# Copying the norms of q and k to SBUF so that GpSimd can scale q and k, with the whole order table replaced

## The chip, the cores and the metric

One core of one Trainium2 chip runs the whole kernel as one program. The metric is the device time of one execution in microseconds; three runs are shown. The engines are named as in the profile: PE (TensorE, with PEld for its weight loads), DVE (VectorE), ACT (ScalarE), POOL (GpSimd) and SP (SyncE, which here only issues DMAs). "f16 pair" below means a float32 value that is held as a float16 part and a float16 rest, so that PE can multiply at float16 speed without losing the precision.

## The reference

Attention over 8 batches, 12 heads, 448 positions and 64 columns, with an RMS norm of q and k ahead of it, then a mixture of experts over the 3584 rows that result.

```
q_n = q / sqrt(mean(q*q, -1) + 1e-6) * g_q        # k_n likewise, with g_k
attn = softmax(q_n @ k_n.T / sqrt(64)) @ v
x = attn as (3584, 768)
group g = argmax(x @ w_group), 4 groups
expert e = argmax(x @ w_expert[g]), 4 in a group
out = softmax weight of g * softmax weight of e * (relu(x @ w1[g, e]) @ w2[g, e])     # inner width 1024
```

## The kernel before

**Work.** Attention runs in 16 units of six heads each (half a batch). A unit's q and k are loaded as 21 blocks of 64 columns on 128 partitions (1344 elements a partition). `plan_prep` prepares a unit: ACT squares (`sq`), DVE sums (`red`, L285), ACT takes the power -1/2 by Ln and Exp (`rs1`, L291 and L292, which writes 42 numbers a partition into PSUM, into unused columns of a bank `po`), DVE refines them by a Newton step (`rs2`, L296 to L298, in the same place). Then DVE multiplies k and q by their norms (`norm`, L301): k in place in two pieces of 896 and 448 elements, q into the buffer `qp` in two pieces of 704 and 640. ACT makes the float16 part of k (`k_hi`, L312), POOL or DVE the rest (`k_lo`, L316, tile `kn`), PE transposes k and q (`pkt` L321, `pqt` L342), and ACT and DVE bring them back to SBUF. The first unit does this in three pieces of 448 (`plan_first`).

`plan_max` finds the row maxima (PE `pmx` L544, DVE `mx` L554), `plan_scores` the scores (PE `pss` L623), their exponentials (ACT `p` L633) and the float16 rest `pl` of each (L639, on POOL or DVE), and `plan_av` multiplies with v (PE `po` L684). Ninety per cent of the 177 `pl` operations take 896 elements. `plan_finish` splits a unit's output into an f16 pair (`xhl`, L751) and stores it.

The second half routes rows to 16 experts and runs them in 18 jobs. An expert's weights are loaded as float32 in 8 pieces of 768 KB (`stage<-w`), split by ACT into a float16 part (`w1h`, `w2h`, L1407) and by DVE into the rest (`w1l`, `w2l`, L1409), and used by PE (`ps` L1458 and L1485). POOL gathers rows (`xg`, L1447), SP transposes them by DMA (`mx<-xg`, L1558).

**What sets the order.** Every step up to the tenth expert job is a task of `Flow`. A table `PLAN` holds one number for each task, in the order in which the tasks are made; tasks are issued in the order of these numbers, and a star picks the second of the engines that the task allows. Each engine then works through its own queue in that order and waits where data, a buffer or a semaphore is missing. The numbers are read for the order alone (and for the places of the later jobs among them).

**One of the two at a time.** Tasks marked by `shared` (L108) are operations of DVE or POOL that read SBUF in a way that the program keeps apart: where a marked DVE task was issued last, the next marked POOL task waits for it by a semaphore (`emit`, L112). It does not make DVE wait for POOL.

Of the kernel before, what the change touches and what calls it, by code (L numbers as in the profile page):

```python
# [59 lines left out]
class Task:  # L60
    def __init__(self, engines, f, deps, takes, uses):
        self.engines, self.f, self.deps, self.takes, self.uses = engines, f, deps, takes, uses
        self.port = False


class Flow:
# [41 lines left out]
    def shared(self, task):  # L108
        task.port = True
        return task  # L110

    def emit(self, agenda, step):  # L112
# [18 lines left out]
class Attention:  # L131
# [7 lines left out]
    ROOM = dict(nk=2, nq=2, nv=2, sq=2, ss=1, qp=1, kn=1, qh=1, kt=3, kb=3, qa=3, qb=3, vh=3, vl=3, mx=2, mxt=2,  # L139
# [121 lines left out]
    def plan_prep(self, flow, u, B, D):  # L261
# [133 lines left out]
        if u == 0:  # L395
            self.plan_first(add, D, B, N, dict(
                sq=sq, red=red, rs1=rs1, rs2=rs2, norm=norm, k_hi=k_hi, k_lo=k_lo, k_tr=k_tr, k_ev=k_ev, k_cp=k_cp, q_one=q_one, q_out=q_out,
                q_dup=q_dup, rms=rms, fl=fl), both, d)
        else:
# [22 lines left out]
            for a, e in HV:  # L422
                n = (e - a) * self.D
                nq.append(add("DVE", lambda a=a, e=e: norm_q(a, e), [y, *nq],
                              takes=[B["qp"]] if a == 0 else (), uses=[B["nq"], B["ss"]] + ([B["qp"]] if a else [])))
# [35 lines left out]
    def plan_first(self, add, D, B, N, F, both, d):  # L461

        fl, rms = F["fl"], F["rms"]
# [10 lines left out]
        for i in range(NPR):  # L474
# [7 lines left out]
            for nm, o in (("k", N), ("q", 0)):  # L482
# [5 lines left out]
            x = add("DVE", (lambda a=a, e=e: F["norm"](fl(d["k"])[:, a:e], fl(d["k"])[:, a:e], rms()[:, N + a:N + e]))  # L488
                    , [y], uses=[B["nk"], B["ss"]])
            nq = add("DVE", (lambda a=a, e=e: F["norm"](fl(d["q"])[:, a:e], fl(d["q"])[:, a:e], rms()[:, a:e])),  # L490
                     [y, x], uses=[B["nq"], B["ss"]])
# [274 lines left out]
    def plan(self, flow, router, order):  # L766
# [15 lines left out]
        for u in range(U):  # L782
            D = {}
            B = {n: Buffer(n, True) for n in ("nk", "nq", "ss", "qp", "kn", "qh")}
# [37 lines left out]
class Router:  # L822
# [177 lines left out]
    def plan(self, flow, a, e, stores, done, room, logits=None):  # L1000
# [5 lines left out]
        d = {}  # L1006
# [95 lines left out]
        for j in range(19):  # L1102
# [3 lines left out]
            x.port = on == "POOL" or j in (1, 3, 5, 6, 12, 15, 18)  # L1106
# [592 lines left out]
1 0 2406 430 1069 2636 9806 12318 12312 708 2073 2 130 550 611 709 710 741 805 1055 1057 1101 1638* 1807 1986 1116  # L1699
1271 1658 1455 2796 210 340 711 792 791 857 922 1181 1296 1402 1362 1775* 1910 2175 1563 1657 3409 1772 4477 612 742  # L1700
864 1056 1054 1115 1180 1272 1349 1561 1562 1912* 2234 2458 1637 1911 2456 2072 4830 1351 2635 4509 2722 4875 2174
# [3 lines left out]
5401 5468 5587 5612 5669 5820 6018 6474 6051 6113 6278 6345 6432 6612 6663 7677 7983* 6943 6944 7033 7275 7277 7367  # L1705
# [4 lines left out]
9606 8050 8174 8337 8404 8539 8598 8743 9184 9577* 8561 8639 9008 9010 9180 9182 9354 9607 10331 9615 9672 10327 10329  # L1710
10336 10340 10344 10744 10805* 11016 11217 12143 2177 2342 2514 2855 2854 3043 3327 3410 3509 3726 3830 3604 3933 4176
3831 4476 4047 4175 4349 4445 6249 4829 4874 4988 5368 5584 5588 5590 5745 5582 5821 7368 7602 10332 7414 7603 7678
8723 8742 9007 7979 8049 8149 8287 8383 8451 8450 8538 8638 7759 7812 9013 9025 9357 9578 9673 10333 10334 10335 10405
9709 9814 10330 10404 10505 10604 10609 10659 10929 10345 10424 10661* 10633 10740 11275 11336 11437 11582 11436 11490
11671 11947 12043 12142 11862 11971 12044 10607 10742 10804 10871 10928 11096 11276 11581 11624 11015 11219 11277
11491 11625 11763 11811 12611 12970* 11910 12045 12316 12374 12460 12594 12706 13497 13668 13684 13980 14761 3832 3178
4054 4523 3812 4828 4832 4915 5108 5467 6162 5204 5585 6434 6049 6433 7035 7113 7617 7756 7320 8540 6734 6841 7034
7031 7032 7278 8289 6942 7676 9440 10346 10660 10605 12372 10328 10337 10338 10965 11218 11220 10342 10347 10606 10754
10831 11017 11221 11235 11335 10608 10741 11585 11761 12313 12384 12500 12969* 12315 12317 12968 12497 12593 12971
12777 12886 13114 12863 12967 13326 12939 13057 13156 13059 13138 13496 13927 14019 14123 14124 14129 14293 14297  # L1720
14465 14620 14519 14577 14760 13498 13670 13674 13676 13680 13687 13771 13978 14296* 13678 13682 13734 13852 14295
14336 14464 14703 15469 14480 14557 14682 14825 14938 15051 15139 15468 15717* 15923 16226 16627 5589 4831 6383 6662
# [10 lines left out]
19906 19563 19565 19860* 17955 18062 18397 18525 18567 18684 18751 19107 19342* 18908 19008 19108 19114 19151 19285  # L1733
# [161 lines left out]
```

## Time and profile before

| | |
|---|---|
| three runs | 983.2, 984.35, 988.45 us; median 984.35 |
| the profiled execution, whole | 988.83 us |
| its span, first to last instruction | 987.1 us |
| PE busy | 899.2 us (91% of the span) |
| DVE busy | 727.5 us (74%) |
| ACT busy | 615.1 us (62%) |
| POOL busy | 540.4 us (55%) |
| mean granted TensorE clock | 0.976 of full speed (2.4 GHz) |

A busy share over the whole span mixes the two halves: attention fills the engines other than PE up to about 470 us, the experts' weights fill the DMA queues after it. So the rows below are by stretch. In a row of the view by stretches each engine's busy time and number of instructions stands first, then the granted clock, the share of the 16 DMA engines and the rate. In a row of the view by groups the numbers after the bar are the busy time of all, the mean of one in ns, and the engine's idle time just before them with what ended it.

### The profile page before, as it was taken

What the parts mean: (1) busy time and instruction counts of PE and PEld (TensorE: products, weight loads), DVE (VectorE), ACT (ScalarE), POOL (GpSimd) and SP (SyncE); (2) the same over time, 40 slices, a digit from 0 to 9 for tenths busy, and PEclk for the clock granted to TensorE, in tenths of its full rate; (3) what the DMA queues carried; (4) which work ended last, traced back from release to release, by engine and by line L of the source; (5) the groups of instructions that cost most, each with busy time, mean ns of one, the idle gap of its engine ahead of it and who ended that gap; (6) DMA issues with size and microseconds to landing.
All of it is one profiled execution on the core that took longest, in us unless ns stands there. A gap on an engine that the chain in (4) does not pass through costs nothing.

```text
span 987.1 us, 28670 instructions
## 1 busy us (share of the span) xinstructions
PE 899.2 (91%) x11761; PEld 647.7 (66%) x11761; DVE 727.5 (74%) x1017; ACT 615.1 (62%) x950; POOL 540.4 (55%) x445
## 2 busy tenths in 40 slices
PE   2789989999998999987989999999879999999997
PEld 2356656666665665655857767667667777878885
DVE  5999989899998999899743656565547685756530
ACT  6779888889988886746441644555426555536521
POOL 7489989989999898677243423112212231424411
PEclk9699999999999999989999999999989999999999
DMA  6775878878789955449999999999988899999920
GB/s 174 186 174 143 204 162 209 165 200 195 191 186 185 222 137 105 113 97 275 240 231 245 279 302 231 286 302 317 252 298 213 299 291 304 323 253 278 293 77 29
DMA packets 222071, 213.82 MB, mean 217 GB/s; under 512 B 128410, under 2 KB 178598, under 8 KB 221937
## 3 DMA queue, kind: packets, MB, share of 16 engines
q1 hardware_dynamic: 213456, 188.46, 74.2%
q0 software_dynamic: 7584, 23.04, 7.5%
q8 instruction: 93, 1.52, 0.7%
q10 hardware_dynamic: 896, 0.46, 0.2%
q14 instruction: 42, 0.34, 0.1%
HBM read 145.69 MB, written 23.41 MB: 171 GB/s over the span
## 4 chain that ended last, share of the span: by engine, by line
PE 37%; DMA 21%; DVE 16%; issue 8%; POOL 6%; ACT 5%; SPq 4%; POOLq 0%; ACTq 0%; DVEq 0%
PE ps L1458 15%; PE ps L1485 12%; DMA mx<-xg 8%; DVE mx L554 5%; POOL pl L639 4%; DMA xg<-x,tb 3%; PE po L684 3%; DMA stage<-w 3%; PE pss L623 3%; ACT p L633 2%; DVE pl L639 2%; DMA qa<-qh 1%; DMA nk<-k 1%; DMA vn<-v 1%; DMA rx<-x 1%
## 5 line engine op out<-in xcount | busy, mean ns | idle before, releaser
L639 POOL TENSOR_TENSOR pl<-p 128x896 f16<-128x896 f32 (+1 forms) x151 | 250.2, 1678 | 38.2 <-ACT p L633 13.9
L1458 PE MATMUL ps<-mx,w1h 128*128 128x256 f16 (+6 forms) x1728 | 246.4, 258 | 18.5 <-DVE hl L1467 9.7
L1458 PE MATMUL ps<-mx,w1l 128*128 128x256 f16 (+6 forms) x864 | 212.3, 258 | 0.0
L554 DVE TENSOR_REDUCE mx<-pmx 128x2 f32<-128x896 f32 (+1 forms) x177 | 174.6, 1033 | 9.5 <-PE pmx L544 6.6
L1458 PEld LDWEIGHTS <-w1h 128*128 128x128 f16 x1728 | 156.2, 99 | 38.3 <-issue 21.9
L633 ACT ACTIVATE p<-pss 128x896 f32<-128x896 f32 (+1 forms) x177 | 152.1, 882 | 46.2 <-PE pss L623 31.8
L684 PEld LDWEIGHTS <-p 128*128 128x128 bf16 (+1 forms) x3072 | 144.1, 102 | 52.3 <-issue 36.8
L684 PE MATMUL po<-vh,pl 128*128 128x65 f16 (+1 forms) x1536 | 156.0, 196 | 15.2 <-POOL pl L639 11.5
L1485 PE MATMUL ps<-w2h,hh 128*128 128x384 f16 (+2 forms) x768 | 163.9, 305 | 3.2 <-ACT y L1497 3.2
L1485 PE MATMUL ps<-w2l,hh 128*128 128x384 f16 (+2 forms) x768 | 163.7, 304 | 0.0
L1485 PE MATMUL ps<-w2h,hl 128*128 128x384 f16 (+2 forms) x768 | 163.5, 304 | 0.0
L684 PE MATMUL po<-vh,p 128*128 128x65 f16 (+1 forms) x1536 | 158.7, 198 | 3.8 <-DVE po L298 1.3
L684 PE MATMUL po<-vl,p 128*128 128x64 f16 (+1 forms) x1536 | 157.1, 194 | 0.0
L1409 DVE SCALAR_TENSOR_TENSOR w2l<-stage,w2h 128x1536 f16<-128x1536 f32 x64 | 111.6, 1752 | 57.6 <-ACT w2h L1407 57.5
L1504 POOL DMA_INDIRECT out<-y,tb x23 | 33.9, 1473 | 215.1 <-ACT y L1497 97.1
L1409 DVE SCALAR_TENSOR_TENSOR w1l<-stage,w1h 128x1536 f16<-128x1536 f32 x64 | 112.9, 1786 | 48.4 <-ACT w1h L1407 48.4
L1485 PEld LDWEIGHTS <-hh 128*128 128x128 f16 (+2 forms) x1536 | 101.2, 100 | 60.6 <-issue 8.3
L684 PEld LDWEIGHTS <-pl 128*128 128x128 f16 (+1 forms) x1536 | 127.5, 102 | 19.1 <-POOL pl L639 14.8
L1465 ACT ACTIVATE hh<-ps 128x256 f16<-128x256 f32 (+6 forms) x144 | 47.4, 348 | 124.2 <-PE ps L1458 107.4
L1407 ACT ACTIVATE w2h<-stage 128x1536 f16<-128x1536 f32 x64 | 94.0, 1478 | 47.3 <-DMA stage<-w 47.3
L1407 ACT ACTIVATE w1h<-stage 128x1536 f16<-128x1536 f32 x64 | 93.4, 1478 | 44.2 <-DMA stage<-w 44.0
L1447 POOL DMA_INDIRECT xg<-x,tb x41 | 57.4, 1401 | 94.6 <-DMA mx<-xg 57.6
(208 smaller groups left out, 1575.6 us busy)
## 6 DMA issues: line engine op xcount, KB each, us to landing
stage<-w SPq DMA_DIRECT2D x64, 768.0 KB
stage<-w SPq DMA_DIRECT2D x64, 512.0 KB
stage<-w SPq DMA_DIRECT2D x64, 256.0 KB
vn<-v SPq DMA_DIRECT2D x16, 576.0 KB
x<-xhl SPq DMA_DIRECT2D x16, 576.0 KB
nk<-k SPq DMA_DIRECT2D x30, 288.0 KB
nq<-q SPq DMA_DIRECT2D x30, 288.0 KB
qa<-qh SPq DMA_DIRECT2D x30, 176.0 KB
```

The source lines that it names most:

```text
L554: nc.vector.tensor_reduce(d["mx"][:, a:ns[-1] + 1:step], d.pop(("mm", a))[:, 0:len(ns), 0:448], axis=AX.X, op=ALU.max)
L623: nc.tensor.matmul(s[:, n - a, 0:448], w[:, n * P:(n + 1) * P], mv[:, x:z], start=first, stop=not first)
L633: nc.scalar.activation(p[:, 0:e - a], s, AF.Exp, scale=1.0 / 64)
L639: ENG[eng].tensor_tensor(l[:, 0:n], p[:, 0:n], h[:, 0:n], op=ALU.subtract)
L684: nc.tensor.matmul(o[op, c, 0:nn], w, mv, start=st, stop=sp, skip_group_check=True)
L1407: self.nc.scalar.activation(hi, t, AF.Copy, scale=64.0)
L1409: self.nc.vector.scalar_tensor_tensor(lo, t, 64.0, hi, op0=ALU.mult, op1=ALU.subtract)
L1447: self.nc.gpsimd.indirect_dma_start(g[0:m], None, self.x16[0:n], bass.IndirectOffsetOnAxis(ap=tb[0:m, i, 0:1], axis=0), bounds_check=n - 1 ...
L1458: nc.tensor.matmul(s[:, 0:c], wb[w][:, i, fs], x[:, l + i, o:o + c], start=i + j == 0, stop=i == DC - 1 and j == 2)
L1465: self.nc.scalar.activation(hh, s[:, 0:c], AF.Relu)
L1485: nc.tensor.matmul(s[q * m:q * m + m, 0:n], self.h[h][:, f, a:a + m], wb[w][:, f, o:o + n], start=f + j == 0, stop=f == self.FC - 1 and j ...
L1504: i = self.nc.gpsimd.indirect_dma_start(out, bass.IndirectOffsetOnAxis(ap=idx, axis=0), d.pop(("y", i))[:, 0:self.D // r], None, bounds_ch ...
```

## The change

**The norms.** After `rs2`, ACT copies the 42 norms from PSUM to a new SBUF tile `z` (`rs3`, 18 copies: one a unit, three in the first). A scaling of q or k may now run on POOL, which multiplies by `z`, or on DVE, which multiplies by the numbers in PSUM as before and does not read `z`. A scaling on POOL waits for the last marked DVE task; a scaling on DVE isn't one that POOL waits for.

```
+    ROOM = dict(nk=2, z=2, ...
...
+        def rs3(a=0, e=N):
+            if "z" not in d:
+                d["z"] = self.wk.tile([P, 2 * N], F32, tag="z", name=f"z{u}", bufs=2)
+            nc.scalar.activation(both_(d["z"], a, e), both_(rms(), a, e), AF.Copy)
+
+        def norm(eng, dst, src, a, z):
+            y = (rms() if eng == "DVE" else d["z"])[:, a:z]
+            ENG[eng].tensor_tensor(dst, src, y.unsqueeze(2).to_broadcast([P, y.shape[1], self.D]), op=ALU.mult)
...
             y = add("DVE", rs2, [x], uses=[B["ss"]])
+            y = add("ACT", rs3, [y], takes=[B["z"]], uses=[B["ss"]])
...
-                nk.append(add("DVE", lambda a=a, e=e: norm_k(a, e), [y], uses=[B["nk"], B["ss"]]))
+                nk.append(flow.shared(add(both[::-1], lambda g, a=a, e=e: norm_k(g, a, e), [y], uses=[B["nk"], B["ss"], B["z"]]), "POOL"))
...
-            if t.port and t.on == "DVE":
+            if t.on == "DVE" and "DVE" in t.port:
                 held[:] = [i for i in seen if i.engine == mybir.EngineType.DVE][-1:]
-            elif t.port and held:
+            elif t.on == "POOL" and "POOL" in t.port and held:
...
 PLAN = """
-1 0 2406 430 1069 2636 9806 12318 12312 708 2073 2 130 550 611 709 710 741 805 1055 1057 1101 1638* 1807 1986 1116
...
```

**What the new table picks.** Twelve of the 66 scalings go to POOL: two of 448 elements in unit 0 (k and q), 448 of k and 704 of q in unit 1, all four in unit 2, 704 of q in units 3 and 8, 640 of q in units 5 and 14. Of `pl`, 11 go from POOL to DVE (nine of 896 elements, two of 448) and 9 from DVE to POOL (eight and one). Of `k_lo`, POOL gains one piece of 448 net. Three outputs `y` of the experts go from ACT to DVE. All other operations stay what they were; nearly all stand in another place.

**POOL, between the first unit's preparation and its first `pl`.** `qp` is the scaled q, `nk` k, `kn` the float16 pair of k, `z` the copied norms; the numbers behind the names (as in `kn_337`) tell buffers apart. Before:

```order
L316 TENSOR_TENSOR kn_337<-nk_237,kn_337 128x14x64
L316 TENSOR_TENSOR kn_337<-nk_237,kn_337 128x7x64
L316 TENSOR_TENSOR kn_474<-nk_320,kn_474 128x14x64
L316 TENSOR_TENSOR kn_474<-nk_320,kn_474 128x7x64
L639 TENSOR_TENSOR pl_0_536<-p_0_535 128x896
```

And in the changed kernel:

```order
L307 TENSOR_TENSOR qp<-nq_254,z_352 128x11x64
L322 TENSOR_TENSOR kn_370<-nk_238,kn_370 128x14x64
L307 TENSOR_TENSOR nk_238<-nk_238,z_352 128x448
L203 MEMSET kb_118 64x1344
L204 MEMSET kb_118 1x1344
L322 TENSOR_TENSOR kn_370<-nk_238,kn_370 128x7x64
L307 TENSOR_TENSOR nk_344<-nk_344,z_446 128x896
L307 TENSOR_TENSOR nk_344<-nk_344,z_446 128x448
L307 TENSOR_TENSOR qp<-nq_332,z_446 128x11x64
L322 TENSOR_TENSOR kn_473<-nk_344,kn_473 128x14x64
L307 TENSOR_TENSOR qp<-nq_332,z_446 128x10x64
L322 TENSOR_TENSOR kn_473<-nk_344,kn_473 128x7x64
```

Two scalings of unit 1 and all four of unit 2 now stand on POOL ahead of its first `pl`, and the second unit's `kn` stands behind three of them.

**DVE, the same place** (`ss` and `po` are `rs2` of unit 2, `mx` a row maximum, `ql` the rest of q). Before:

```order
L298 SCALAR_TENSOR_TENSOR po_112<-ss_392,po_112 128x42
L554 TENSOR_REDUCE mx_347<-pmx_20_434 128x1
L301 TENSOR_TENSOR nk_320<-nk_320,po_112 128x896
L301 TENSOR_TENSOR nk_320<-nk_320,po_112 128x448
L354 SCALAR_TENSOR_TENSOR ql_437<-pqt_1_451,ghc,qh_436 128x384
L301 TENSOR_TENSOR qp<-nq_339,po_112 128x11x64
L554 TENSOR_REDUCE mx_347<-pmx_16_469 128x2
```

And now:

```order
L298 SCALAR_TENSOR_TENSOR po_112<-ss_419,po_112 128x42
L563 TENSOR_REDUCE mx_368<-pmx_20_425 128x1
L360 SCALAR_TENSOR_TENSOR ql_444<-pqt_0_428,ghc,qh_443 128x1024
L360 SCALAR_TENSOR_TENSOR ql_444<-pqt_1_448,ghc,qh_443 128x384
L563 TENSOR_REDUCE mx_368<-pmx_14_467 128x2
```

The three scalings between `rs2` and the next row maximum are gone from DVE.

**DVE, where attention ends** (`pl15_18` is the `pl` of the last unit's blocks 18 and 19, `w1l0` the rest of the first expert's weights, `roh`, `rd`, `rc` and `rq` belong to the router). Before:

```order
L1409 SCALAR_TENSOR_TENSOR w1l0_9555<-stage3_9562,w1h0_9554 128x1536
L1046 TENSOR_TENSOR roh21_10036<-rd21_9812 128x48
L1409 SCALAR_TENSOR_TENSOR w1l0_9555<-stage1_9560,w1h0_9554 128x1536
L639 TENSOR_TENSOR pl15_18_10034<-p3215_18_10033 128x896
L1409 SCALAR_TENSOR_TENSOR w1l0_9555<-stage0_9559,w1h0_9554 128x1536
```

And now:

```order
L648 TENSOR_TENSOR pl15_10_9873<-p3215_10_9872 128x896
L1047 SCALAR_TENSOR_TENSOR rc21_9846<-rd21_9844,prio_219 128x60
L1418 SCALAR_TENSOR_TENSOR w1l0_9488<-stage0_9492,w1h0_9487 128x1536
L1418 SCALAR_TENSOR_TENSOR w1l0_9488<-stage3_9495,w1h0_9487 128x1536
L1049 TENSOR_REDUCE rcm21_9847<-rc21_9846 128x15
...
L1055 TENSOR_TENSOR roh21_10066<-rd21_9844 128x48
L648 TENSOR_TENSOR pl15_16_9982<-p3215_16_9981 128x896
L1068 TENSOR_TENSOR rq21_10120<-prr21_10076,roh21_10066 128x48
L648 TENSOR_TENSOR pl15_18_10027<-p3215_18_10026 128x896
L1418 SCALAR_TENSOR_TENSOR w1l0_9488<-stage1_9493,w1h0_9487 128x1536
```

Two `w1l` still stand ahead of the last `pl` on DVE, now both further ahead, and `pl15_16` has come from POOL to stand between.

## Rows read from the trace of the kernel before

**Rows 1.** Busy time by stretch (us): PE, PEld, DVE, ACT, POOL; clock, DMA share, GB/s.
```profile
8.00:48.00 40.00, 23.66 (x129) 14.21 (x130) 37.30 (x58) 31.53 (x46) 20.14 (x34) 0.79 0.81 198
48.00:440.00 392.00, 362.78 (x6171) 239.99 (x6170) 368.32 (x535) 320.42 (x555) 345.11 (x253) 0.99 0.73 168
440.00:470.00 30.00, 24.17 (x481) 17.80 (x478) 28.69 (x43) 19.95 (x31) 20.57 (x23) 0.94 1.00 246
470.00:700.00 230.00, 219.19 (x2443) 165.88 (x2442) 131.34 (x191) 110.78 (x157) 71.83 (x60) 0.99 0.99 273
700.00:764.00 64.00, 54.05 (x431) 40.98 (x430) 37.93 (x41) 29.04 (x35) 13.62 (x11) 0.92 0.86 248
```

**Rows 2.** Groups by form, whole span: the moved operations and their nearest relatives.
```profile
L639 POOL TENSOR_TENSOR pl<-p 128x896 f16<-128x896 f32 x136 | 235.3, 1749 | 34.5 <-ACT p L633 13.1 <-DVE vl L392 7.2 <-DVE pl L639 4.3
...
L316 POOL TENSOR_TENSOR kn<-nk,kn 128x896 f16<-128x896 f32 x14 | 26.6, 1898 | 8.8 <-PE pmx L544 7.8 <-ACT kn L312 0.9
...
L316 POOL TENSOR_TENSOR kn<-nk,kn 128x448 f16<-128x448 f32 x16 | 18.1, 1134 | 7.4 <-ACT kn L312 4.1 <-issue 2.3 <-ACT rl L1024 0.9
...
L301 DVE TENSOR_TENSOR nk<-nk,po 128x896 f32<-128x896 f32 x15 | 16.2, 1081 | 0.2
...
L639 POOL TENSOR_TENSOR pl<-p 128x448 f16<-128x448 f32 x15 | 15.4, 1028 | 3.7 <-DVE pl L639 2.9 <-ACT p L633 0.8
...
L301 DVE TENSOR_TENSOR qp<-nq,po 128x704 f32<-128x704 f32 x15 | 13.2, 877 | 0.0
...
L301 DVE TENSOR_TENSOR qp<-nq,po 128x640 f32<-128x640 f32 x15 | 12.2, 811 | 0.0
...
L301 DVE TENSOR_TENSOR nk<-nk,po 128x448 f32<-128x448 f32 x18 | 10.9, 610 | 0.7 <-ACT po L292 0.6
...
L292 ACT ACTIVATE po<-y 128x42 f32<-128x42 f32 x15 | 3.1, 209 | 0.6 <-PE po L684 0.2
```

**Rows 3.** Chain of waits, 38 to 48 us: start, us, what ended last.
```profile
38.70 0.61 DVE nk L301
...
39.84 0.80 DVE qp L301
...
43.60 1.51 PE pkt L321 x14
```

**Rows 4.** DVE in order of time, 24 to 41 us: start, us, operation.
```profile
25.90 0.88 DVE L301 TENSOR_TENSOR qp<-nq,po 128x704 f32<-128x704 f32 x1
26.70 0.61 DVE L301 TENSOR_TENSOR nk<-nk,po 128x448 f32<-128x448 f32 x1
...
37.06 0.21 DVE L298 SCALAR_TENSOR_TENSOR po<-ss,po 128x42 f32<-128x42 f32 x1
```

**Rows 5.** POOL in order of time, 27 to 48 us; in brackets, idle time before.
```profile
39.91 2.88 POOL L316 TENSOR_TENSOR kn<-nk,kn 128x896 f16<-128x896 f32 x2 [7.79 <-PE pmx L544]
```

**Rows 6.** Chain of waits, 60 to 200 us: the moved scalings on it.
```profile
63.77 0.87 DVE qp L301
...
194.96 0.14 DVE qp L301
```

**Rows 7.** PE's waits, 48 to 440 us (first row) and 440 to 470 us (others): total, times, longest.
```profile
PE po L684 <- POOL pl L639: 7.6, 17, 1.3
...
PE po L684 <- POOL pl L639: 3.9, 4, 2.1
PE po L684 <- DVE pl L639: 2.0, 2, 1.6
```

**Rows 8.** DVE in order of time, 456 to 463 us.
```profile
455.92 3.25 DVE L1409 SCALAR_TENSOR_TENSOR w1l<-stage,w1h 128x1536 f16<-128x1536 f32 x1
...
460.70 1.74 DVE L1409 SCALAR_TENSOR_TENSOR w1l<-stage,w1h 128x1536 f16<-128x1536 f32 x1
462.37 1.08 DVE L639 TENSOR_TENSOR pl<-p 128x896 f16<-128x896 f32 x1
```

**Rows 9.** ACT, SP's queue and POOL in order of time, 442 to 459 us.
```profile
451.30 1.48 ACT L1407 ACTIVATE w1h<-stage 128x1536 f16<-128x1536 f32 x1
...
457.02 1.74 ACT L633 ACTIVATE p<-pss 128x896 f32<-128x896 f32 x2
...
442.67 0.39 SPq L1393 DMA_DIRECT2D stage<-w  x1
...
454.24 3.32 POOL L639 TENSOR_TENSOR pl<-p 128x896 f16<-128x896 f32 x2 [0.23 <-DVE rr L689]
```

**Rows 10.** Chain of waits, 430 to 560 us: the experts' first matmuls.
```profile
468.48 8.27 PE ps L1458 x72
```

More of the change, by code (lines that the diff above doesn't have):

```diff
@@ L62, in __init__ @@
         self.engines, self.f, self.deps, self.takes, self.uses = engines, f, deps, takes, uses
-        self.port = False
+        self.port = ""
 class Flow:
@@ L106, in order, with shared @@
         return sorted(self.tasks, key=lambda t: t.start)
-    def shared(self, task):
-        task.port = True
+    def shared(self, task, on="POOL DVE"):
+        task.port = on
         return task
@@ L131 @@
 class Attention:
-    ROOM = dict(nk=2, nq=2, nv=2, sq=2, ss=1, qp=1, kn=1, qh=1, kt=3, kb=3, qa=3, qb=3, vh=3, vl=3, mx=2, mxt=2,
+    ROOM = dict(nk=2, z=2, nq=2, nv=2, sq=2, ss=1, qp=1, kn=1, qh=1, kt=3, kb=3, qa=3, qb=3, vh=3, vl=3, mx=2, mxt=2,
                 psd=3, psx=2, pso=2, p=7, xm=1, hl=1, rx=2, rl=1,
@@ L395, in plan_prep @@
         if u == 0:
-            self.plan_first(add, D, B, N, dict(
-                sq=sq, red=red, rs1=rs1, rs2=rs2, norm=norm, k_hi=k_hi, k_lo=k_lo, k_tr=k_tr, k_ev=k_ev, k_cp=k_cp, q_one=q_one, q_out=q_out,
+            self.plan_first(flow, D, B, N, dict(
+                sq=sq, red=red, rs1=rs1, rs2=rs2, rs3=rs3, norm=norm, k_hi=k_hi, k_lo=k_lo, k_tr=k_tr, k_ev=k_ev, k_cp=k_cp, q_one=q_one, q_out=q_out,
                 q_dup=q_dup, rms=rms, fl=fl), both, d)
@@ L423, in plan_prep @@
                 n = (e - a) * self.D
-                nq.append(add("DVE", lambda a=a, e=e: norm_q(a, e), [y, *nq],
-                              takes=[B["qp"]] if a == 0 else (), uses=[B["nq"], B["ss"]] + ([B["qp"]] if a else [])))
+                nq.append(flow.shared(add(both[::-1], lambda g, a=a, e=e: norm_q(g, a, e), [y, *nq], takes=[B["qp"]] if a == 0 else (),
+                                          uses=[B["nq"], B["ss"], B["z"]] + ([B["qp"]] if a else [])), "POOL"))
             kt = []
@@ L459, in plan_prep, with plan_first @@
                                           uses=[B["nv"], B["vh"]] + ([B["vl"]] if a else []))))
-    def plan_first(self, add, D, B, N, F, both, d):
+    def plan_first(self, flow, D, B, N, F, both, d):
+        add = flow.add
         fl, rms = F["fl"], F["rms"]
@@ L487, in plan_first @@
             y = add("DVE", pair(F["rs2"], a, e), [x], uses=[B["ss"]])
[L488 to L491, printed above, removed]
+            y = task("z", "ACT", pair(F["rs3"], a, e), [y], takes=[B["z"]], uses=[B["ss"]])
+            x = flow.shared(add(both[::-1], (lambda g, a=a, e=e: F["norm"](g, fl(d["k"])[:, a:e], fl(d["k"])[:, a:e], N + a, N + e)),
+                                [y], uses=[B["nk"], B["ss"], B["z"]]), "POOL")
+            nq = flow.shared(add(both[::-1], (lambda g, a=a, e=e: F["norm"](g, fl(d["q"])[:, a:e], fl(d["q"])[:, a:e], a, e)),
+                                 [y], uses=[B["nq"], B["ss"], B["z"]]), "POOL")
             x = task("kh", "ACT", pair(F["k_hi"], a, e), [x], takes=[B["kn"]], uses=[B["nk"]])
@@ L783, in plan @@
             D = {}
-            B = {n: Buffer(n, True) for n in ("nk", "nq", "ss", "qp", "kn", "qh")}
+            B = {n: Buffer(n, True) for n in ("nk", "nq", "ss", "z", "qp", "kn", "qh")}
             B.update({n: Buffer(n, u % 3 != (U - 1) % 3) for n in ("kt", "kb", "qa", "qb")})
@@ L1105, in plan @@
                     takes=[bp] if j == 7 else (), uses=[bp] if j == 8 else [rl] if j < 2 else ())
-            x.port = on == "POOL" or j in (1, 3, 5, 6, 12, 15, 18)
+            x.port = on if on == "POOL" or j in (1, 3, 5, 6, 12, 15, 18) else ""
         self.puts.append([add("POOL", lambda j=j: put(j), [x]) for j in range(n)])
@@ new lines @@
+23297 23405 23558 23560 23841 24258 24736 24779* 23839 23938 24138 24283 24526 24660 24781 24987 25250* 25256 25313
+25356 25469 25582 25672 25754 26076 26438 26806 26929 27672 15507 14983 16290 16420 16016 16554 16805 17205 17227
+17488 17841 19398 17719 18407 18971 18827* 19065 19608 19878 19908 20124 21125 20571 20713 20878 20812 20876 20936
+21374 21539 20877 21537 23837 23557 25310 22444 22631 22697 22738 22808 22908 23239 23383 23561 24377 24460 24573
+23576 23937 24037 23559 23577 24707 24780 24843 25506 25624 25795 25311 25312 25470 25411 25489 25776 25836 26079
@@ new lines @@
+57094 59489 59533 58020 59519 59659 58540 59660 59692 59534 59620 59919 59619 59921 60091 59768 60097 60397 59918
+60067 60249 60070 60217 60399 60470 60880 61168 61757* 62535 61756 62916* 64822 56914 57287 58151 58676 58772 59180
+57092 58254 59080 57634 58153 59082 59182 59920 59923 59924 60396 60882 60098 60545 61504 58154 59922 60881 55374
+56177 58021 58671 59661 58675 59520 59081 60398 62006 62303 61167 62053 62298 61503 62100 62534 62300 62446 62807
+62447 62809 63166 62532 62810 62866 62805 63078 63215 63167 63352 63412 63481 63891 64000 64423 65214 64438 65217*
@@ new lines @@
+64820 65954* 66063 65340 66614 67666 60069 60247 60410 60546 61166 62806 60099 62148 62533 60250 62808 63079 62101
+63547 64127 62054 62297 63462 62304 63125 65751 62305 64274 64437 57095 60100 62299 61170 62302 60251 63351 65750
+65810 63871 65809 65853 65210 65779 66060 65730 65879 65923 65880 66058 66410 66062 66583 66613 66178 66507 66551
+66328 66477 66582 66723 67279* 67275 68770* 69219 67868 68199 68774 63892 64125 65215 63413 63483 65752 64275 65212
+65780 65213 65341 66061 64821 65924 66329 66413 68100 68104 65216 66412 67277 65854 66088 66722 59693 62448 63463
@@ L1840 @@
+73045 73454* 73545
 """
```

149 lines of the change are left out of this document (72 added, 77 removed), and 127 rows, old and new, of the table PLAN.

## The prediction

> **What bounds the kernel now.** I first cut the span into stretches [rows 1], because attention and the experts have different limits. From 48 to 440 us four engines are nearly full: of 392 us PE is busy 362.78, DVE 368.32, POOL 345.11, ACT 320.42. None alone sets the time; each is fed by the others through a few buffers, so taking work off one gives back a part of it only. From 8 to 48 us it is different: DVE is busy 37.30 of 40 us, POOL 20.14 and PE 23.66, so the start hangs on DVE and POOL has room. From 470 to 700 us PE is busy 219.19 of 230 us and the DMA share is 0.99; what attention gives up earlier reaches the end only if weights are loaded earlier too. From 700 to 764 us PE has its largest hole of the second half, 10 us, at a granted clock of 0.92, that is, partly at 1.2 instead of 2.4 GHz.
>
> Then the groups by form [rows 2] give prices, and the chain of waits shows which scalings stand where the time is made. Two of the twelve that leave DVE stand on it in the start [rows 3] and two in the middle [rows 6]. Last come PE's waits [rows 7] and the engines in order of time where attention ends [rows 8, 9]: there PE stands still for `pl`, 5.9 us in 30.
>
> **The change part by part.** The sum is made against the profiled execution (988.83 us, 4.48 above the median of 984.35) and then set off from the median.
>
> *Totals.* Off DVE go four scalings of 448, one of 896, four of 704 and three of 640: 4 x 0.610 + 1.081 + 4 x 0.877 + 3 x 0.811 = 9.5 us [rows 2]. No row shows a scaling on POOL. The nearest is `kn` there, which like it reads two SBUF operands: 1134 ns for 448 elements and 1898 for 896, 1.705 ns an element more. That puts 704 at 1.57 and 640 at 1.46 us, as an estimate, and the twelve at 4 x 1.134 + 1.898 + 4 x 1.57 + 3 x 1.46 = 17.1 us, against 345 us of POOL work in the middle.
>
> *The start, -1.0 us.* Eight of the twelve lie before POOL's first `pl`: two of unit 0, two of unit 1, all four of unit 2. The two of unit 1, 0.88 and 0.61 us, ran ahead of unit 2's `rs2`, which ended at 37.27 us [rows 4]; without them it ends at about 35.8. Now comes the copy to `z` at about the price of ACT's 42-number operation, 0.21 us [rows 2], so POOL can begin unit 2 at 36.1: k 1.90 and 1.13, q 1.57, then the first `kn` 1.90. That is ready at 42.6 us. PE's transposes of it began at 43.60, on the chain [rows 3]: 1.0 us gained. DVE alone would give more, the 0.88 and 0.61 ahead of `rs2` and the 0.61 and 0.80 on the chain, 2.9 us; what is late next is POOL, which does in 6.5 us what DVE and POOL did side by side. Bounds: -2.9, and +1.0 if POOL reaches unit 2 two microseconds late, since it has two scalings of unit 0 (2.27 us), two of unit 1 (2.70) and two fills ahead. Its cover is the 7.79 us that it idled before unit 2's `kn` [rows 5].
>
> *The copies, 0.* Fifteen of 42 numbers and three smaller, 18 x 0.21 = 3.8 us of ACT at most, which idles 72 us from 48 to 440 [rows 1]. A scaling on DVE doesn't read `z` and doesn't wait for it. If ACT's idle time were always elsewhere, it would cost the 3.8.
>
> *The middle, -0.6 us.* On the chain stood 0.87 and 0.14 us of scalings that now run on POOL [rows 6]: -1.0. POOL gets four late scalings, 2 x 1.57 + 2 x 1.46 = 6.1 us, and a `kn` of 448, 1.1; it gives up, net, one `pl` of each size, 1.75 + 1.03 [rows 2]: +4.4 us on an engine that idles 47 us of 392. PE waited for POOL's `pl` 7.6 us in 17 places [rows 7], short waits: POOL runs just ahead of need. I take a tenth of the 4.4 us, about POOL's idle share, as felt: +0.4. Bounds: 0 and +4.4. What the rest of the new order does here can't be read from rows; PE's own idle time, 29 us, is the ceiling, and I put it at 0.
>
> *The end of attention, -1.7 us.* The last `pl` on DVE could have begun when `p` was done, at 457.02 + 1.74 = 458.8 us, and began at 462.37, behind `roh` and a `w1l` of 1.74 us [rows 8, 9]; POOL's last `pl` waits for it by the semaphore, and PE for that. In the new order that `w1l` stands behind the `pl`, and the two that are still ahead split the weights that are loaded first. I take the 1.74. Bounds: nothing, and all 5.9 us of PE's waits for `pl` there [rows 7].
>
> *The experts, 0.* Same operations but for three outputs from ACT to DVE, which both idle half of the time there. Earlier loads pass the gain on; PE's holes of 10.8 and 10.0 us [rows 1] say how far a new order of loads and gathers could move it either way.
>
> Sum: -1.0 - 0.6 - 1.7 = -3.3 us, 985.5 for the profiled execution and **981.0 us** from the median. A measurement of this kernel can't tell less than about 0.5% (4.9 us) from no change, so this forecast counts as no change.
>
> **The rivals.**
>
> *Both ends pay in full, 975.1 us.* The start gives 2.9, the middle 0.4 and the end of attention 5.9: -9.2. For it: these are waits that rows show, and the new order frees DVE at the right places. Against it: POOL is next in line in the start. Decides: whether PE's waits for `pl` after 440 us are gone.
>
> *The experts' loads set the end, 984.4 us.* With a DMA share of 0.99 from 470 to 700 us, an earlier end of attention is idle time of PE later, if the first weights are not asked for earlier. Against it: PE is busy 95% there, so it isn't waiting much.
>
> *Weights hold up the last scores, slower, 992.2 us.* In the new order two `w1l` stand ahead of the last two `pl` on DVE, and POOL's last three `pl` come behind marked DVE tasks that stand behind them. Before, the first load was asked for at 442.67 and `w1h` began at 451.30, after the `p` of its time [rows 9]. If attention arrives earlier than the weights, ACT's `p` and DVE's `pl` stand behind a DMA. Price: two `w1l` at the 3.25 us that the first one took [rows 8], 6.5 us, and up to 3 of waiting for the landing, less the 1.6 of start and middle: +7.9. It decides from where the first load is issued less than 8.6 us ahead of its split.
>
> *POOL and DVE keep each other from SBUF, 987.0 us.* The first `w1l` took 3.25 us where the next took 1.74, while POOL ran two `pl` in 3.32 us [rows 8, 9]; so one such meeting costs DVE 1.5 us. A scaling on DVE reads one operand in PSUM, one on POOL reads both in SBUF. If each of the four late ones meets such a DVE operation on the chain, 6.0 us are lost on 981.0. The program makes only POOL wait for DVE, so nothing keeps DVE from starting into a POOL operation. The Trainium skill says so too ("SBUF — State Buffer", section "SBUF: two separate sides"): the port pair that both use is an exclusive lock, and a DVE operation with two SBUF inputs and a GpSimd operation keep each other out for a whole instruction. The two rows of the trace agree with that.
>
> **How the numbers follow.** The forecast has 0.36, both ends paying 0.33, the loads setting the end 0.12, the meetings on SBUF 0.06, the weights ahead of the last scores 0.13. So faster by over 0.5% (under 979.4) has 0.33, within 0.5% 0.36 + 0.12 + 0.06 = 0.54, and slower (over 989.3) 0.13. The range that holds it 8 times in 10 takes in the first rival and 1.6 us below it for the holes of the second half, 973.5, and reaches up to 989.5, so that most of the slow case is left out. The likeliest case alone spans 979.4 to 984.
>
> **What would show it.** In the profile after: DVE's scalings down to 54 and 12 on POOL of 1.1 to 1.9 us; the transposes of unit 2 near 42.6 us; POOL busier by 15 us and DVE less by some 8 before 470 us; PE's waits for POOL's `pl` not above 10 us from 48 to 440; and the first `ps` of the experts 3 us before 468.48 [rows 10]. I am wrong if that first `ps` comes at the same time or later, if the last `pl` still stand behind `w1l` that wait for weights, or if it comes 3 us earlier and the end does not.

## The result and the profile after

The changed kernel takes 993.41 us (median of eleven; 986.77 to 1005.39) against 986.51 us (982.06 to 992.99) for the kernel before, measured together: a ratio of 1.0069, 95% interval 1.0045 to 1.0092. Without its one execution in a slower state, 1005.39 us, its median is 992.2, 5.7 us over the kernel before. Measured a second time (run 13) the ratio was 1.0056 (1.0023 to 1.0089). So it is slower by about 0.6%, some 6 us. The forecast was 981.0, the same within 0.5%, and its range ended at 989.5: wrong, and on the other side.

The two profiled executions differ less, 990.94 against 988.83 us: the first lies 2.5 us under its median, the second 2.3 over. So a trace shows here where time goes, and the medians show how much.

The changed kernel by stretches (columns as in [rows 1]):

```profile
8.00:48.00 40.00, 26.30 (x141) 14.38 (x142) 36.37 (x54) 32.70 (x54) 30.52 (x37) 0.96 0.74 188
48.00:440.00 392.00, 363.50 (x6198) 240.61 (x6196) 367.22 (x536) 321.15 (x558) 351.85 (x261) 0.99 0.76 169
440.00:470.00 30.00, 23.06 (x438) 16.19 (x439) 21.54 (x34) 19.18 (x29) 18.35 (x17) 0.89 0.97 244
470.00:700.00 230.00, 219.03 (x2442) 165.84 (x2440) 134.05 (x195) 109.78 (x159) 73.46 (x61) 0.99 0.94 274
700.00:764.00 64.00, 53.37 (x415) 39.84 (x413) 35.56 (x38) 30.57 (x34) 10.93 (x9) 0.89 0.82 256
```

From 8 to 48 us PE does 2.6 us more than in [rows 1] and POOL 10.4 more, at a granted clock of 0.96 instead of 0.79: the start is ahead. From 440 to 470 us every engine does less than before, DVE by 7 us, at a granted clock of 0.89 instead of 0.94: there the engines wait for each other. The moved scalings, by form (columns as in [rows 2]):

```profile
L307 POOL TENSOR_TENSOR qp<-nq,z 128x704 f32<-128x704 f32 x4 | 5.5, 1365 | 0.4 <-POOL vh L188 0.4
...
L307 POOL TENSOR_TENSOR nk<-nk,z 128x448 f32<-128x448 f32 x3 | 2.8, 937 | 2.5 <-ACT z L303 2.5
```

The twelve cost POOL 14.7 us instead of the estimated 17.1. The end of attention in the chain of waits (start, us, what ended last):

```profile
450.98 1.46 POOL xg L1456
452.45 0.97 issue
453.42 2.19 POOL pl L648
455.61 0.05 issue
455.66 0.56 PE po L693 x7
...
461.58 1.23 PE po L693 x41
462.81 2.00 issue
464.81 0.30 POOLq L1389
465.11 1.91 POOL pl L648
467.02 0.05 issue
467.06 1.53 PE po L693 x52
468.60 0.43 PE ps L1467 x3
```

A gather of the experts' rows, `xg`, stands on the path that sets the end of attention. POOL in order of time tells why (in brackets, idle time before):

```profile
444.51 0.67 POOL L1434 DMA_DIRECT2D tb<-tab  x1 [1.42 <-issue]
445.28 1.67 POOL L648 TENSOR_TENSOR pl<-p 128x896 f16<-128x896 f32 x1
450.98 2.40 POOL L1456 DMA_INDIRECT xg<-x,tb  x1 [4.03 <-DVE rc L1047]
453.42 2.18 POOL L648 TENSOR_TENSOR pl<-p 128x896 f16<-128x896 f32 x1
```

and SP's queue, which asks for the experts' weights:

```profile
440.93 0.39 SPq L1402 DMA_DIRECT2D stage<-w  x1
441.52 0.35 SPq L1403 DMA_DIRECT2D stage<-w  x1
442.07 1.22 SPq L1399 DMA_DIRECT2D stage<-w  x1
443.48 0.33 SPq L1400 DMA_DIRECT2D stage<-w  x1
444.00 0.33 SPq L1399 DMA_DIRECT2D stage<-w  x1
444.53 0.33 SPq L1400 DMA_DIRECT2D stage<-w  x1
```

POOL asks at 444.51 us for the list of rows, `tb`, and the gather needs it. Its semaphore counts up for the last time at 450.71, 6.2 us later; POOL stands in the gather until then, with the `pl` of blocks 8 and 9 behind it, whose `p` was done by 449.1. PE waits for that `pl` 4.8 us. The profile names DVE's `rc` as the releaser, but `rc` only happened to end at 450.71 too: in a second profile the same wait is 5.7 us and "ended" by DVE's `w1l`, and in the first experiment by the DMA of `tb`. In the kernel before, two of the six load instructions were asked for ahead of `tb` instead of five and the sixth with it, `tb` landed after 4.1 us, and POOL was in a `pl` until 0.16 us before the gather began. PE's waits there (total, times, longest; before in [rows 7]):

```profile
PE po L693 <- POOL pl L648: 7.1, 3, 4.8
```

A second thing is in the chain: the last `pl` on POOL (465.11) is released by the last `pl` on DVE, which stood behind the routing's `rq`, and `rq` waited 3.2 us for PE's `prr`.

### The profile page after: what moved, and what is told of

It reads as the page before. It is cut to its first block, busy times and chain, and to the rows that moved or that the text cites. A ratio compares the mean times of both kernels' runs of the same rounds, so it can differ in the third digit from the quotient of the medians.

```text
span 989.2 us, 28715 instructions
## 1 busy us (share of the span) xinstructions
PE 902.6 (91%) x11761; PEld 647.3 (65%) x11761; DVE 719.5 (73%) x1008; ACT 617.9 (62%) x966; POOL 556.2 (56%) x456
## 4 chain that ended last, share of the span: by engine, by line
PE 51%; DVE 16%; DMA 11%; ACT 8%; POOL 6%; issue 5%; SPq 2%; ACTq 0%; POOLq 0%; DVEq 0%
PE ps L1494 20%; PE ps L1467 19%; DMA stage<-w 5%; DVE mx L563 5%; PE po L693 4%; PE pss L632 4%; POOL pl L648 3%; ACT p L642 2%; DMA nk<-k 1%; DVE w2l L1418 1%; DVE ss L285 1%; DVE vl L398 1%; ACT kt L333 1%; DVE pl L648 1%; PE pss L627 1%
## 5 line engine op out<-in xcount | busy, mean ns | idle before, releaser
L648 POOL TENSOR_TENSOR pl<-p 128x896 f16<-128x896 f32 (+1 forms) x149 | 245.1, 1664 | 29.6 <-ACT p L642 14.2
L1467 PEld LDWEIGHTS <-w1h 128*128 128x128 f16 x1728 | 155.4, 98 | 34.8 <-issue 14.7
```

The source lines that it names most:

```text
L648: ENG[eng].tensor_tensor(l[:, 0:n], p[:, 0:n], h[:, 0:n], op=ALU.subtract)
L1467: nc.tensor.matmul(s[:, 0:c], wb[w][:, i, fs], x[:, l + i, o:o + c], start=i + j == 0, stop=i == DC - 1 and j == 2)
```

## The experiments

Runs 1 to 4 share a chip; so do 5 to 8, 9 to 12, 13 to 16, and 17 and 18. A ratio is always to the kernel before on the same chip (medians 985.2, 985.8, 992.4, 983.8 and 985.2 us). Theory S puts the loss at the end of attention, theory E into the new order of the experts, theory P into the scalings on POOL, theory C into the copies. Numbers of the order table are written as `PLAN[task]`.

**1. The end of attention, mended by three numbers.**

```
-PLAN[2227] = 44020; PLAN[2225] = 44353; PLAN[2113] = 45245
+PLAN[2227] = 44176; PLAN[2225] = 44674; PLAN[2113] = 45296
```

> The changed kernel, three numbers of its table altered: POOL's first two gathers go behind the scores' pl of blocks 8-9 and 12-13 of unit 15, and the routing's rq on DVE goes behind the pl of blocks 18-19. Theory S (the time is lost where attention ends: POOL stands in a gather that waits for its list, 4.0 us, with a pl behind it that PE waits for, up to 4.8 us; and DVE stands 3.2 us in rq with the last pl behind it): PE's first expert ps comes 4 to 6 us before 468.6, and the kernel gains 3 to 6 us on the changed one, ratio to the kernel before 1.001 to 1.004. Theory E (the time is lost in the new order of the experts' half): ps may come earlier but the end stays at a ratio of 1.007. Theory P (the scalings on POOL cost it): no change at the seam or at the end.

Measured 1.0081 (1.0053 to 1.0109). POOL's last `pl` ended at 463.8 instead of 467.0, but the first `ps` came at 471.20, later than 468.60. The chain of this run says why:

```profile
459.25 5.34 DMA xg<-x,tb
464.59 0.02 issue
464.61 6.46 DMA mx<-xg
471.07 0.14 issue
471.20 4.00 PE ps L1467 x18
```

The second gather now came too late, and landing and transposing its rows took 11.8 us. A wait was exchanged for another one; this says nothing on S.

**2 to 4. Attention, its end and the experts, each from the one or the other order.**

```
-t.start, t.on = new table
+t.start, t.on = new table if new number < 430 (run 2) or < 470 (run 3) else old table
+t.start, t.on = old table if old number < 470 else new table; no scaling on POOL (run 4)
```

> The changed kernel up to 430 of the table's numbers (attention with its copies and the twelve scalings on POOL), and the order of the kernel before from there on: the end of attention and the experts. Theory S and theory E both give a gain here, since attention runs 2 to 3 us ahead at 430 us and neither seam nor experts are new: ratio to the kernel before 0.996 to 0.999. Theory P (scalings on POOL cost): 1.003 to 1.007, as in the changed kernel.

> The changed kernel's order up to 470, so with its end of attention, and the experts' order of the kernel before from there on. Theory S: the loss is already made at 470, so a ratio of 1.004 to 1.008. Theory E: the loss is gone, 0.997 to 1.001.

> The order of the kernel before up to 470, all scalings on DVE (the copies to SBUF are made, nobody reads them), and the changed kernel's order from there on. Theory S: nothing is lost, 0.998 to 1.002. Theory E: the whole loss, 1.004 to 1.009.

Measured: 1.0025 (1.0000 to 1.0050) with new attention and the old rest, 1.0061 (1.0029 to 1.0092) with the new end of attention added, 1.0086 (1.0057 to 1.0114) with old attention and the new experts. Run 2 falls between the ranges: S and E had both promised a gain. Runs 2 and 3 differ by the end of attention alone: 3.6 us, with intervals that overlap. In run 2 PE waits for POOL's `pl` there as long as before, in place of 7.1 us:

```profile
PE po L693 <- POOL pl L648: 3.9, 4, 2.1
```

Run 4 has the median that theory E asked for, but its trace shows otherwise: it is 6.4 us behind the kernel before at the last `mx` of attention, 7.0 at the last `p` and 6.3 at the last `hh` of the program (`hh` is the float16 part of an expert's inner values, written by ACT, and `hl` the rest, written by DVE). In this trace the experts lose nothing; the old attention with eighteen unread copies does. A median that fits doesn't make a theory right.

**5, 13. The kernel before and the changed kernel once more.** No edit.

> The kernel before once more, for a second profile of it. Theory V (the first profile of before, 4.5 us over the median, was late already in attention, so that the 1 to 4 us by which the new attention leads it are partly the first profile's own): the last maximum mx of attention on DVE, at 435 us in the first profile, is 1 to 3 us earlier here. Theory not-V (attention runs alike each time, and the runs differ in the experts): within 0.7 us of it.

> The changed kernel once more, on the chip of the next three runs, so that its parts are compared on one chip, and for a second profile of it. If the first measurement holds: 1.005 to 1.009 of the kernel before. Attention as in the runs with the same order: the last mx on DVE between 2.6 us ahead and 1 us behind the kernel before, the last p 4 to 5 us behind it.

The second profile of before (988.66 us) has the last `mx` 0.4 us earlier than the first: theory V falls, the lead of the new attention is real. The second profile of the changed kernel (990.22 us) has it 1.1 us ahead of before, the first 2.6; the last `p` is 6.9 us behind, in the first 4.4. So 7 to 8 us are lost between the two, in both. `tb` took 7.8 us to land in the second.

**6, 7. Fewer copies; the order alone.**

```
 def rs3(a=0, e=N):
+    if u not in (0, 1, 2, 3, 5, 8, 14) or (u == 0 and a == 14): return   # run 6
+    return   # run 7, and no scaling starred for POOL
```

> The changed kernel with only those copies to SBUF that a scaling on POOL reads: units 0 (two of three), 1, 2, 3, 5, 8 and 14; ten copies are gone, nothing else is altered. In the program the first scaling of each unit on DVE waits for ACT's copy, though it reads PSUM. Theory C (that wait costs): the kernel gains 2 to 5 us on the changed one, ratio to the kernel before 1.002 to 1.005, and DVE's scalings wait for ACT's copy less than 1 us in all. Theory S (the copies are free, the loss is at the end of attention): 1.006 to 1.008.

> The changed kernel's order with no copies and all scalings on DVE, so the new order alone. Theory C and theory P (copies, or scalings on POOL, cost): 0.998 to 1.003 of the kernel before. Theory S (the order loses at the end of attention whatever is scaled where): 1.005 to 1.009; DVE has 9.5 us more to do, and if the twelve scalings on POOL were worth what was forecast, it is 1 to 3 us slower than the changed kernel, 1.008 to 1.010.

Run 6: 1.0032 (1.0000 to 1.0065), within what theory C asked for, yet its last `mx` is 1.6 us behind before where run 8, on the same chip with all copies, is 0.4 ahead. Attention didn't get faster, so the median can't be put down to the copies; run 6 is inconclusive. Run 7: 1.0115 (1.0080 to 1.0150), its last `mx` 7.5 us behind. In an order made for scalings on POOL, having them there is worth some 8 us of attention (run 8 against run 7): theory P falls.

**8, 16. The end of attention mended with both gathers early, under the new and the old experts.**

```
-PLAN[2227] = 44020; PLAN[2225] = 44353; PLAN[2113] = 45245
+PLAN[2227] = 44176; PLAN[2225] = 44177; PLAN[2113] = 45296
```

> As the first run (rq on DVE behind the pl of blocks 18-19), but both of POOL's first gathers stand directly behind the pl of blocks 8-9 and ahead of that of 12-13, since in the first run the second gather was issued at 459.2 and its data, landed and transposed at 471.1, held up the first expert. Theory S: first ps at 464 to 467 us against 468.6 in the changed kernel, and the ratio to the kernel before 1.002 to 1.005. If the experts' half takes the gain back, the end stays at 1.006 to 1.008.

> The third run (new attention and new end of attention, old experts) with the gathers and rq placed as in the eighth. Theory S (the end of attention loses about 4 us, of which these three numbers give back 3): 1.001 to 1.004 of the kernel before, where the third run had 1.006. If the loss at the end of attention lies elsewhere: 1.005 to 1.008.

Measured 1.0040 (1.0015 to 1.0065) and 1.0070 (1.0040 to 1.0099). PE's waits for POOL's `pl` fell to 2.3 us in both, and the first `ps` came at 467.2 and 466.5. But `rq` and the gathers were not the last in line. ACT in run 8:

```profile
472.57 1.48 ACT L1416 ACTIVATE w2h<-stage 128x1536 f16<-128x1536 f32 x1 [8.53 <-DMA stage<-w]
```

ACT stands 8.5 us in a split for a load that SP asks for behind the transposes, and the first `hh` stands behind it: it begins at 476.8, in the changed kernel at 473.2. The two runs don't agree on a gain, and none is claimed.

**9, 10. The copies alone, and the scalings on POOL, in the old order.**

```
+18 tasks rs3, each right behind its rs2; order otherwise the old table's   # run 9
+the twelve scalings starred for POOL; only the copies that POOL reads   # run 10
```

> The order of the kernel before with the eighteen copies to SBUF added and nothing else: all scalings stay on DVE and read PSUM. Theory C (the first scaling of a unit waits for ACT's copy, and ACT for DVE's rs2): attention ends 4 to 7 us later than before, ratio 1.004 to 1.007. The forecast on record (the copies cost 0, 3.8 us at most): 0.999 to 1.002.

> The order of the kernel before with the twelve scalings on POOL, at their places in that order, and only the eight copies that these read. Theory X (the scalings on POOL pay by themselves, some 8 us between the run of the order alone and the run with the needed copies, and the new order is what loses): 0.992 to 0.998 of the kernel before. Theory Y (they pay only in an order that is made for them, POOL being late with kn and pl in the old one): 1.002 to 1.010.

Run 9: 1.0063 (1.0030 to 1.0096), the last `mx` 4.9 us late. Who stands for the copies there (us, times; in the second fence total, times, longest):

```profile
  DVE nk L307: 4.1, 6
```

```profile
DVE rr L698 <- ACT z L303: 1.1, 2, 0.8
DVE xm L717 <- ACT z L303: 0.9, 1, 0.9
```

These scalings run on DVE and read PSUM, not `z`, and still they wait for ACT's copy: 16 of DVE's scalings carry a wait on ACT in this program, 6 before. So do `rr` and `xm`, which take no norms and read the output of attention in the bank `po`, where the norms lie. Run 10: 1.0128 (1.0072 to 1.0185), the last `mx` 6.4 us late. That is above theory Y's range and far from X's: the scalings by themselves don't pay in the old order, as Y said.

**11, 12. All mended parts together; new attention with fewer copies.**

```
 PLAN as in run 8, rs3 as in run 6
-PLAN[2197] = 45353; PLAN[2188] = 46381
+PLAN[2197] = 44889; PLAN[2188] = 44890
```

> The changed kernel with only the copies that POOL reads, the gathers and rq placed as in the eighth run, and on SP the loads of the first w2 pieces (0,7,3 and 0,4,0) ahead of the transposes of the gathered rows, since in the eighth run ACT stood 8.5 us in the split of such a piece, with the first hh behind it. Theory S+C (the three are separate losses of 2 to 4 us): 0.994 to 0.999 of the kernel before. If the experts' half takes it back: 1.000 to 1.004.

> As the second run (new attention up to 430, then the old end of attention and the old experts), with only the copies that POOL reads. Theory C: 2 to 4 us under the second run, 0.997 to 1.000 of the kernel before. Theory S alone: as the second run, 1.001 to 1.004.

Measured 1.0087 (1.0049 to 1.0126) and 1.0047 (1.0013 to 1.0080). Both expectations missed. On this chip `p` falls back by 6 to 9 us between 414 and 424 us in all four runs, and some 2 to 4 us of it are left at the last `mx`. So the traces of 11 and 12 aren't laid beside the others, and of the 4.9 and 6.4 us of runs 9 and 10 only 2.6 and 4.1 were there at 415 us. In the medians removing copies shows no gain (1.0047 against run 2's 1.0025, with intervals that overlap). With run 6 inconclusive, theory C has no support in the new order; it isn't refuted.

**14, 15, 18. The start alone.** New order up to 60 (run 14) or 50 (15, 18), with the eight scalings of units 0 to 2 on POOL, and the old order from there.

```
-t.start, t.on = new table
+t.start, t.on = new table if new number < 60 (or 50) else old table
+rs3 and scalings on POOL for units 0, 1 and 2 only
```

> The changed order up to 60 of the table's numbers with the eight scalings of units 0 to 2 on POOL and their five copies, and from there the order of the kernel before, with all scalings on DVE and no copies: the start of the change by itself. Theory A (the start is a true gain of about 2 us, as at 59 us in all runs of the new order, and nothing behind it gives it back): the last mx of attention 1.5 to 3 us ahead, ratio 0.996 to 0.999. Theory B (units 0 to 2 done earlier leave the rest waiting for the same engines): the lead is under 1 us at 435 us, ratio 0.999 to 1.002.

> As the run before, with the seam between the two orders at 50 instead of 60, so that the result does not hang on where they are joined. Theory A: 0.996 to 0.999. Theory B: 0.999 to 1.002.

> The run of the start alone, joined at 50, once more: its profile led by 6.6 us at the end of attention and by 8.5 at the end of the program, while its median was 0.7 us above that of the kernel before (0.9991 of it, 0.9962 to 1.002). If the start's 2.8 us at 59 us are kept and reach the end: 0.994 to 0.998. If the experts' half takes them back in most runs: 0.998 to 1.001.

Measured 1.0030 (0.9994 to 1.0067), 0.9991 (0.9962 to 1.0020) and 1.0000 (0.9969 to 1.0032), so none has the gain of theory A in its median. In the profiles of runs 15 and 18 the last `mx` is 6.6 and 3.4 us ahead: the start's gain lasts through attention. At the end it can't be measured. Runs 15 and 18 are one kernel, and the first was 8.0 us faster at the end in its profile, the second at par with before. Their stretches from 515 to 545 us, run 15 first:

```profile
515.00:530.00 15.00, 14.31 (x141) 10.05 (x141) 1.99 (x6) 2.26 (x6) 5.86 (x7) 1.00 0.99 269
530.00:545.00 15.00, 14.66 (x368) 12.65 (x366) 7.44 (x15) 7.78 (x15) 6.99 (x6) 1.00 0.88 216
```

```profile
515.00:530.00 15.00, 10.19 (x98) 8.40 (x98) 6.70 (x10) 1.69 (x5) 10.10 (x7) 1.00 0.76 190
530.00:545.00 15.00, 15.00 (x246) 10.72 (x245) 1.19 (x6) 1.36 (x5) 4.94 (x7) 0.89 1.02 245
```

In run 18 PE waits 3.4 us for transposed rows and then runs at 0.89, that is, for a part at 1.2 GHz: its lead of 4.6 us at 520 is 0.5 us of lateness at 536.

**17. One load of weights later.** The changed kernel; SP asks for the weights' piece 0,1,1 behind the write of unit 14's rows.

```
-PLAN[2179] = 43855
+PLAN[2179] = 44353
```

> The changed kernel, one number altered: SP's load of the weights' piece 0,1,1 goes from ahead of the write of unit 14's rows to behind it, so that POOL's first list tb is asked for behind four load instructions instead of six (the kernel before has two, and there tb landed 4.1 and 4.0 us after it was asked for; the changed kernel in two profiles 6.2 and 7.8). Theory L (the list is late because of the loads in front of it, and POOL stands in the gather for the list): tb lands 4.5 to 5.5 us after it is asked for, PE's waits for POOL's pl from 440 to 470 us fall from 7.1 and 7.7 us to 4 to 6, and the kernel gains 1 to 3 us on the changed one: 1.003 to 1.006 of the kernel before. If the landing has another cause: 6 us or more, and no gain.

Measured 1.0014 (0.9985 to 1.0042): 987.35 us, 4 to 5 us under the changed kernel by either of its ratios; the interval lies under that of the first and overlaps that of the second. POOL in order of time:

```profile
445.62 0.66 POOL L1434 DMA_DIRECT2D tb<-tab  x1 [1.41 <-DVE rr L699]
446.31 1.70 POOL L648 TENSOR_TENSOR pl<-p 128x896 f16<-128x896 f32 x1
449.69 1.66 POOL L1456 DMA_INDIRECT xg<-x,tb  x1 [1.69 <-DMA tb<-tab]
451.38 1.78 POOL L648 TENSOR_TENSOR pl<-p 128x896 f16<-128x896 f32 x1
```

and PE's waits:

```profile
PE po L693 <- POOL pl L648: 3.1, 3, 1.5
PE pss L632 <- ACT p L642: 1.8, 1, 1.8
PE po L693 <- ACT xm L713: 1.7, 1, 1.7
PE po L693 <- DVE pl L648: 1.0, 2, 0.6
```

`tb` lands 3.8 us after it is asked for, the gather waits 1.7 us instead of 4.0, PE waits 3.1 us in all for POOL's `pl` instead of 7.1 and 7.7. Theory L holds for the list, more strongly than expected. Two things keep it from being the whole story. The late load now holds up ACT's next split (3.9 us, with two `p` behind it). So PE's waits from 440 to 470 us still add up to 7.6 us (7.1 and 8.7 in the changed kernel), and the first `ps` comes at 469.2, no earlier than in the first profile of the changed kernel and 1.9 us before that of the second. And 4 to 5 us of the gain come between the first `hh` and 545 us. There the changed kernel loses time in both profiles: DVE stands in a `w2l` (the rest of a piece of `w2`) for weights, with `hl` behind it, and PE waits for `hl` (longest 3.8 and 3.4 us; 1.8 in the kernel before):

```profile
518.07 1.76 DVE L1418 SCALAR_TENSOR_TENSOR w2l<-stage,w2h 128x1536 f16<-128x1536 f32 x1 [3.63 <-ACT hh L1474]
```

ACT had waited 3.45 us for that piece's load, and the clock was 0.89 from 515 to 530 us. In run 17 the loads were asked for 1.8 us earlier, PE's longest wait for `hl` was 1.6 us and the clock 1.00. How the one load that was moved, at 444 us, brings this about was not shown step by step.

## Why the prediction was wrong, by its own steps

**Right:** *the totals.* Before 470 us DVE does 8.6 us less than before and POOL 14.7 more; forecast were some 8 and 15. (In the second pair of profiles, runs 13 and 5, it is 2.8 and 13.2.)

**Right in their sum, by luck in the parts:** *the start, -1.0, and the middle, -0.6.* The last `mx` of attention came 2.6 and 1.1 us ahead, forecast 1.6. But the start gave more than forecast. POOL began unit 2 at 36.10 us, as forecast, its scalings were cheaper, and PE's transposes of it began at 41.90, forecast 42.6, in the second profile at 40.74. The two `p` that began at 62.61 us before begin at 59.98 and 60.27, a lead of 2.6 and 2.3. The step had no term for the clock, which in both profiles of before was granted at 0.79 from 8 to 48 us and now at 0.96 and 0.91; what part of the lead is the clock's no run shows. So the middle gave nothing in one profile and lost 1.2 us in the other, though PE waited 7.5 us for POOL's `pl` there, 7.6 before [rows 7].

**Without harm seen in this order, on a wrong ground:** *the copies, 0.* "A scaling on DVE doesn't read `z` and doesn't wait for it" is half wrong. It doesn't read `z`, but copy and scaling read the same bank of PSUM from two engines, and the program lets the scaling wait for the copy. In the old order that costs 6.4 us of attention in run 4, over the bound of 3.8, which counted ACT's busy time alone; run 9's `p` are late alike until 380 us (5.0 us, run 4 5.3). In the new order DVE's scalings wait 2.2 us in three places, and ten copies fewer show no gain that can be told from noise (runs 6 and 12). The Trainium skill, "PSUM — Partial Sum Buffer", section "PSUM bank collisions raise a hardware error", says why a program has such waits: a ScalarE read and a VectorE read that overlap in one bank and the same partitions raise an error, and the compiler's scheduler adds a dependency between any two instructions on different engines that touch the same bank there, reads and writes alike. The waits of run 9 agree with the dependency; the error no run here shows.

**Wrong:** *the end of attention, -1.7 us.* This is the step that failed. From the last `mx` to the first `hh` the changed kernel loses 4.8 and 5.9 us against before, its first `ps` comes at 468.60, not 3 us before 468.48, and runs 2 and 3 put 3.6 us of the total there. The other traces agree: the eight further profiles with the new order of this stretch lose 3.4 to 7.8 us in it (runs 1, 3, 6, 7, 8, 11, 16, 17), the eight further ones with the old order -0.6 to 1.1 (runs 2, 4, 9, 10, 12, 14, 15, 18). The step looked at DVE's `pl` behind `w1l`. It didn't follow the POOL queue: there a gather was moved ahead of a `pl`, and the list it waits for was asked for behind three pieces of weights instead of one, so it landed after 6.2 and 7.8 us instead of 4.1. In run 17, with a piece less in front, it landed after 3.8. The Trainium skill, "DMA: Bandwidth & Descriptors", section "Issuing engines are not separate DMA queues", says that DMAs of SP and GpSimd run on the same 16 engines and interleave; the landings agree. But run 17 still loses 5.4 us from the last `mx` to the first `hh`: with the list on time, the split of the late piece and a split of `w2` (ACT waited 3.9 and 5.0 us for their loads) are next in line. That the new order of this stretch costs time is shown, and that the list made POOL and PE wait; how the loss divides between the list, the loads and `rq` stays open.

**Wrong in part:** *the experts, 0.* The new order alone costs nothing there (run 4 goes from 7.0 us behind to 6.3). But the bound of "±10 for holes" was where leads went: with one hole of PE at 516 to 532 us and the clock behind it, 4.6 us of lead are gone in run 18, and the changed kernel loses 3.4 and 3.3 us at its hole between 516 and 526 us in its two profiles.

**The rivals.** "Weights hold up the last scores" had 992.2 us and a chance of 0.13, and 993.41 came. Its sign and price were right. Its mechanism, two `w1l` that stand for their weights, was not: the first two `w1l` waited for no load. The weights held up POOL's list. The rival's own condition was met by a little, without its consequence: the first load was asked for 8.2 us ahead of its split (440.93 and 449.12 us), less than the 8.6 named, and the split waited for nothing. That its price came so near is luck. The meetings of POOL and DVE in SBUF show no price: DVE's `pl` of 896 elements took 1196 ns in the mean, 1294 before.

What stays open: the medians differ by some 6 us and the pairs of profiles by 2 (990.94 and 990.22 against 988.83 and 988.66), so some 4 us of the loss are in no trace. Run 17 gives back 4 to 5 us by one load, but by which way is not shown. Both profiles of before are slower than its median, and what its faster executions do better no trace shows. And none of the eighteen runs beats the kernel before clear of noise: the start alone is level with it (0.9991 and 1.0000).

## What to carry to other kernels

When an order is changed, walk every in-order queue, also the one that issues DMAs: a small DMA whose result an engine waits for in its own queue is better asked for ahead of bulk loads (2.9 us against 6.2 and 7.8 here), or the wait put behind the work that others need. Removing a wait without looking at what is next in line (the second gather in run 1, the splits of weights in runs 8 and 17) exchanged one stall for another three times here. And read a median only together with the place in the trace where it is made; run 4 had the right number for a theory that its trace refutes.

## What the runs showed that was not expected

- The landing of one 2 KB list went with what was asked for just before it: 2.9 us with no load in front (run 2), 3.4 to 5.5 with two or three of the six load instructions (the kernel before twice, 4.1 and 4.0, and runs 4, 9, 10, 12, 14, 15 and 18), 3.8 with four, the last of them 1.8 us ahead (run 17), and 5.2 to 8.0 with five or six (the changed kernel twice, runs 1, 3, 6, 7, 8, 11 and 16). The groups touch, so the count alone doesn't settle it.
- A hole of PE in the first experts can be paid twice, but need not be. In the profiles of runs 8, 16 and 18 PE stood 3.4 to 3.9 us between 525 and 532 us, and the granted clock from 530 to 545 us was 0.89, that is, partly 1.2 instead of 2.4 GHz. In both profiles of before and in runs 2, 15 and 17 PE stood there 1.9 us at most, and it was 1.00. But run 1 stood 3.4 us just before 533 and kept 1.00, as run 2 did after 2.9 us at 517. The same kernel fell on either side in two profiles (runs 15 and 18).
- On POOL an f32 product of two SBUF operands took 937 ns for 448 elements a partition, 1365 for 704 and 1687 for 896, less than its `kn` with an f16 operand and result (1134 and 1898 [rows 2]).
